# Weight loads of a two-layer attention kernel issued in the order of their readers, with the static plan of all engines drawn up anew

## The chip, the core and the metric

The kernel runs on one core of one Trainium2 chip. The metric is the device time of the whole program in microseconds (us). A core has five engines that each work through their own instruction list in order: TensorE (PE in the profile; its weight loads are PEld), ScalarE (ACT), VectorE (DVE), GpSimd (POOL) and SyncE (SP). ACT, POOL and SP also issue DMA transfers; what they spend on that is listed as ACTq and SPq, and for POOL as an operation of POOL.

## The reference, cut to what matters

```python
def attention(x, mem0, Wq, Wk, Wv, Wo, seg_len):      # x: 2048 x 512, 64 segments of 32 rows
    mem = mem0                                         # 8 x 512
    for s in range(64):
        h = concat([mem, x[segment s]])                # 40 x 512
        q, k, v = h @ Wq, h @ Wk, h @ Wv               # 32 heads of 128
        p = softmax(where(mask, q @ k.T * 128**-0.5, -1e9))
        o = (p @ v) @ Wo                               # 40 x 512
        mem = o[:8]; out += [o[8:]]
    return concat(out)
x = x + attention(layernorm(x), mem0, ...)
x = x + relu(layernorm(x) @ w1) @ w2                   # 512 -> 1376 -> 512
x = x + attention(layernorm(x), mem0, ...)             # the same weights again
x = x + relu(layernorm(x) @ w1) @ w2
```

All weights and activations are bf16, sums are f32. The segments of one layer depend on each other through `mem`, eight rows that come out of the output projection of the segment before.

## The kernel before

**Tiling and stages.** Both attention layers run at once, the second four segments behind the first (DELTA = 4), so the program has 68 steps. Step k works on segment k of the first layer and segment k-4 of the second; 80 columns hold both. A step projects queries and keys (L906, 128x128 weight tiles against 80 columns, or 40 where only one layer is active), values (L826, or L845 where only one layer is active), forms scores (L935), takes the softmax on DVE and ACT (L946 to L976), transposes the probabilities on PE (L532, `P`), copies them out twice with a mask (L999 on ACT, L1001 on DVE), multiplies with the values (L1018) and projects with Wo (L1045). L1061 copies the eight memory rows into the input `HT` of the next step. Every second step a pair of segments is finished: residual, layer norm and the dense layer (L532 and L641), as work that fits between the rest.

**Start.** All weights stay in SBUF. Wv is loaded in parts of 1, 1 and 2 MB, and Wq, Wk and Wo in two halves of 2 MB each: 16 MB. One 1 MB part of Wv is issued from SP, the eight other loads from POOL (L388, L391). While they land, PE works on groups of 128 rows of x: `prepare_group` loads a group (L678, from ACT for groups 1 to 5), normalizes it and computes its values (`late_values`), which are parked in the room of the dense weights (`w_sb` in the profile) and put to DRAM (`vh`, L802). The normalized group is put to DRAM too (`xh`, L686, from SP). `hold` (L397) is a tiny DMA from SP that reads the last head of Wo_sb; most DMAs of SP stand behind it ("loaded"), so that they do not compete with the weights.

**What sets the order.** Nothing is scheduled by hand. `Plan` records every operation with a cost for each engine that can do it, what it reads and writes, and for DMAs a lag until the data are there. `Plan.order` then simulates the engines and picks at each point, among the operations that could start soon, the one with the best priority: for PE operations `PERIOD * step + PLACE[...]`, for the rest the priority of their readers less cost, latency and `AHEAD[...]`. RULE holds four numbers of the picking rule. PLACE and AHEAD are tables of numbers found by a search. The result is one fixed list of instructions per engine. A transpose or attend operation marked EITHER is issued as one 128-column or as two 64-column matmuls, whichever leaves PE in the column mode it is in.

**How waits come about.** The framework that builds the program puts semaphore waits in front of instructions. Each DMA issued from SP or ACT signals one of eight completion semaphores, given out in turn in the order in which the program lists these DMAs. Before a DMA may use a semaphore again, its issuing engine waits until the DMA that had it before has landed. DMAs from POOL have eight semaphores of their own.

Of the kernel before, what the change touches and what calls it, by code (L numbers as in the profile page):

```python
# [24 lines left out]
       (0.13, 0.13, 0.10, 0.10, 0.20, 0.0), (1.7, 1.7, 1.7, 1.7, 1.7, 0.0), (0.3, 0.3, 0.3, 0.3, 0.3, 0.0))  # L25
# [4 lines left out]
RULE = (0.0406, 305.8805, 223.7607, 5137528097.847)  # L30
PERIOD = 51.862
PLACE = {
    ("attend.mmu0.0", 0): 464.738, ("attend.mmu0.0", 1): -761.84, ("attend.mmu1.0", 0): -48.299,
    ("attend.mmu1.0", 1): 477.592, ("attend.mmu2.0", 0): -121.389, ("attend.mmu2.0", 1): 193.039,
    ("attend.mmu3.0", 0): 108.108, ("attend.mmu3.0", 1): -173.388, ("attend.mmu4.0", 0): -138.04,
    ("attend.mmu4.0", 1): -86.354, ("dense_layer.mm.0", 1): 703.986, ("dense_layer.mm.1", 1): 23.772,
    ("dense_layer.mm.2", 1): 450.741, ("dense_layer.mm.3", 1): 440.377, ("dense_layer.mm.4", 1): 333.982,
    ("dense_layer.mm.5", 1): 738.493, ("finish_pair.turn.0", 1): 163.159, ("g0", 0): -34.469, ("g1", 0): 381.157,
    ("g2", 0): -795.105, ("g3", 0): 5.833, ("g4", 0): 32.661, ("g5", 0): 203.205, ("layernorm.turn.0", 1): 205.098,
    ("layernorm.turn.1", 1): 314.469, ("layernorm.turnr.0", 0): -1.427, ("prepare.turns.0", 0): 41.19,  # L40
    ("project.mm.0", 0): 149.221, ("project.mm.0", 1): 441.958, ("project.mm.1", 0): 706.274,
    ("project.mm.1", 1): 331.02, ("project.mm.2", 0): 669.447, ("project.mm.2", 1): 820.125,
    ("project.mm.3", 0): -204.869, ("project.mm.3", 1): -13.931, ("project.mm.4", 0): -186.279,
    ("project.mm.4", 1): -181.007, ("queries_keys.mmu0.0", 0): 5.896, ("queries_keys.mmu0.0", 1): -44.155,
    ("queries_keys.mmu0.1", 0): 34.674, ("queries_keys.mmu0.1", 1): -93.489, ("queries_keys.mmu0.2", 0): -16.377,
    ("queries_keys.mmu0.2", 1): 173.172, ("queries_keys.mmu0.3", 0): 19.391, ("queries_keys.mmu0.3", 1): -750.374,
    ("queries_keys.mmu1.0", 0): 17.611, ("queries_keys.mmu1.0", 1): -732.885, ("queries_keys.mmu1.1", 0): -106.018,
    ("queries_keys.mmu1.1", 1): -97.778, ("queries_keys.mmu1.2", 0): 41.801, ("queries_keys.mmu1.2", 1): -156.695,
    ("queries_keys.mmu1.3", 0): -179.942, ("queries_keys.mmu1.3", 1): 16.276, ("queries_keys.mmu2.0", 0): 291.119,
    ("queries_keys.mmu2.0", 1): 294.131, ("queries_keys.mmu2.1", 0): 91.208, ("queries_keys.mmu2.1", 1): 35.615,  # L50
    ("queries_keys.mmu2.2", 0): 163.031, ("queries_keys.mmu2.2", 1): 388.265, ("queries_keys.mmu2.3", 0): 189.92,
    ("queries_keys.mmu2.3", 1): 152.536, ("queries_keys.mmu3.0", 0): 82.328, ("queries_keys.mmu3.0", 1): 396.443,
    ("queries_keys.mmu3.1", 0): 54.307, ("queries_keys.mmu3.1", 1): 465.336, ("queries_keys.mmu4.0", 0): 414.302,
    ("queries_keys.mmu4.0", 1): 455.006, ("queries_keys.mmu4.1", 0): 428.286, ("queries_keys.mmu4.1", 1): 697.474,
    ("scores.mmu0.0", 0): -184.452, ("scores.mmu0.0", 1): 31.061, ("scores.mmu1.0", 0): 330.969,
    ("scores.mmu1.0", 1): -683.203, ("scores.mmu2.0", 0): -29.182, ("scores.mmu2.0", 1): -711.846,
    ("scores.mmu3.0", 0): 189.271, ("scores.mmu3.0", 1): -735.95, ("scores.mmu4.0", 0): -722.578,
    ("scores.mmu4.0", 1): 229.19, ("scores.turnu0.0", 0): 31.636, ("scores.turnu0.0", 1): 404.707,
    ("scores.turnu1.0", 0): 487.486, ("scores.turnu1.0", 1): -33.575, ("scores.turnu2.0", 0): 202.144,
    ("scores.turnu2.0", 1): -88.841, ("scores.turnu3.0", 0): -183.584, ("scores.turnu3.0", 1): -17.909,  # L60
    ("scores.turnu4.0", 0): 67.36, ("scores.turnu4.0", 1): 309.356, ("values.mm.0", 0): -186.102,
    ("values.mm.0", 1): 27.498, ("values.mm.1", 0): 32.826, ("values.mm.1", 1): 183.35,
    ("values.mm.2", 0): -107.199, ("values.mm.2", 1): 352.654, ("values.mm.3", 0): 428.105,
    ("values.mm.3", 1): -12.855, ("values.mmv0.0", 0): -89.763, ("values.mmv1.0", 0): 182.482,
    ("values.mmv2.0", 0): -173.822, ("values.mmv3.0", 0): 303.007, ("values_narrow.mm.0", 0): 182.487,
    ("values_narrow.mm.0", 1): -707.928, ("values_narrow.mm.1", 0): 164.081, ("values_narrow.mm.1", 1): -54.214,
}
AHEAD = {
    "*bulk.land": -65.074, "*late_values.put": 329.507, "*layernorm.aggr": -154.03, "*layernorm.keep": 171.765,
    "*layernorm.norm": 293.888, "*layernorm.power": 209.943, "*layernorm.stats": -173.956,  # L70
    "*prepare_group.load": -399.388, "*prepare_group.put": 280.114, "*values.ev": -52.264, "attend.ev": -169.821,
    "bulk.land": -92.619, "dense_layer.relu": 31.743, "dense_layer.relu_last": 127.159, "finish_pair.add": -113.115,
    "finish_pair.add0": -180.166, "finish_pair.add1": -44.709, "finish_pair.store": 305.649,
    "finish_pair.widen": 141.765, "late_values.put": -48.547, "layernorm.aggr": -189.08, "layernorm.keep": 259.017,
    "layernorm.norm": 2.975, "layernorm.power": 143.261, "layernorm.stats": 94.33, "load_dense.dma1": -95.621,
    "load_dense.dma2": 105.989, "load_group.get": 80.276, "load_group.load": -149.366, "load_weights.dma": -58.491,
    "load_weights.hold": 85, "make_ident": 333.562, "make_mask": -62.557, "place_values.dma": -76.842,
    "prep_x.cp": -213.044, "prepare.get_memory": -66.381, "prepare.get_x": 46.124, "prepare.keep": 225.327,
    "prepare.make_half": -61.416, "prepare.place": -66.003, "prepare.zero": 321.465, "prepare.zero_bank": -109.711,
    "prepare.zero_columns": 238.474, "prepare_group.load": 103.093, "prepare_group.put": 27.159,  # L80
    "project.ev": 229.927, "project.first": 257.853, "project.rows": -8.657, "queries_keys.ev": 381.586,
    "scores.block": 258.34, "scores.exp": -22.515, "scores.keep": 353.957, "scores.mul": 275.286,
    "scores.recip": -213.702, "scores.sub": 91.821, "scores.top": -68.377, "scores.total": 68.935,
    "values.ev": 156.514, "values_narrow.ev": -13.151,
}

LOAD, LOAD_O = 2.55, 2.9
# [8 lines left out]
def t_act(n):  # L96
    return 0.05 + 0.833e-3 * n
# [6 lines left out]
PART = {ACT: 0.13, DVE: 0.10}  # L104
# [193 lines left out]
def kernel(  # L298
# [74 lines left out]
    def bulk(eng, t, fn, name, size, r=(), w=(), rate=LOAD):  # L373

        def land():
            pass

        plan.op(eng, t, fn, r=r, w=[("issued", *name)], lag=1.5)
        plan.op(QUEUE, rate * size, land, r=[("issued", *name)], w=[*w, "queue"])
# [91 lines left out]
    def prepare():  # L471
# [34 lines left out]
        plan.available("memory", 5.0)  # L506
# [44 lines left out]
    def layernorm(x, rows, xnT, lo=0, n=128, to=None, halved=False):  # L551
# [37 lines left out]
        plan.op(POOL, 0.65, power, r=["half"], w=[ln])  # L589
# [5 lines left out]
    def dense_layer(x, rows, act):  # L595
# [4 lines left out]
        for fb in range((NFC + 3) // 4):  # L600
# [27 lines left out]
            if nfull < len(fcs):  # L628
                copy_op(n, relu_last, r=[hp], w=[hT, (hT, fb)], part=True)
# [38 lines left out]
    def prepare_group(g, gate=()):  # L668

        eng, q, t, cond = queue(g <= EARLY)  # L670
        if g == 0:
            xb = xb_tiles[0]
            plan.available(xb0, 4.0)
        else:
            xb = p_xe.buf()

            def load():
                q.dma_start(out=xb[:, :], in_=A_x[0, 128 * g:128 * (g + 1), :])  # L678

            plan.op(eng, t, load, r=[*cond, *gate], w=[xb], lag=3.5 if g <= EARLY else 2.45)  # L680
# [85 lines left out]
    def copy_op(n, fn, r, w, part=False):  # L766
        plan.op((ACT, DVE), (t_act(n) + part * PART[ACT], t_dve(n) + part * PART[DVE]), fn, r=r, w=w)
# [88 lines left out]
    def place_values(k, late):  # L856
# [6 lines left out]
        if late:  # L863
            src, key = (vg, [("vg", p) for p in range(4)]) if g == 0 else (vh[g], [("vh", g, 0), ("vh", g, 2)])
            for b in range(2):
                def dma(b=b):
                    q.dma_start(out=V0[64 * b:64 * b + HS, :, :], in_=src[64 * b + HS * c:64 * b + HS * (c + 1), :, :])

                plan.op(eng, t, dma, r=[*cond, *key], w=[("V0l", b)], lag=2.45)
            return  # L870
        for u in range(2):
            for b in range(2):
# [8 lines left out]
                plan.op(eng, t, dma, r=[*cond, *[("vw", i) for i in range(4)[src]]], w=[("V0", i, b) for i in ps], lag=2.45)  # L881
# [36 lines left out]
    def scores(k, p, xs, a_lo, a_hi, qk):  # L918
# [75 lines left out]
        for b in range(2):  # L994
# [8 lines left out]
            copy_op(n, keep, r=[tp, PT, "half"], w=[(PT, b)])  # L1003
# [175 lines left out]
```

## Time and profile before

| what | value |
|---|---|
| time, median of 3 runs | 1670.47 us (1670.08 to 1671.12) |
| the profiled execution's own time | 1670.9 us |
| its span, first to last instruction | 1669.2 us |
| mean granted TensorE clock | 0.992 |
| PE busy | 1605.1 us, 96% of the span, 40146 matmul records |
| PEld, DVE, ACT, POOL busy | 82%, 66%, 63%, 10% |
| DMA | 64.26 MB, mean 38 GB/s |

PE is busy 96% of the span, so a microsecond of PE work or of PE waiting is a microsecond of the result, save where the start or the end of the program is bound by transfers. Because matmuls overlap in the array, the busy share alone doesn't show how densely they follow each other; the time from the start of one matmul to the start of the next does. "Position" below means the sum of these start-to-start times along PE's instruction list, without any waiting: for 80 columns 36 ns, for 40 columns 25 ns, for 512 columns 216 ns (two 64-column matmuls share one such slot), and 96 ns more at each change between 128-, 64- and 32-column mode. All are medians of this trace.

### The profile page before, as it was taken

To read this page: it belongs to the slowest core of one execution; us is meant where nothing else is said; L and a number is where in the kernel's file an instruction comes from. 1 tells how busy PE (TensorE), PEld (TensorE's weight loads), DVE (VectorE), ACT (ScalarE), POOL (GpSimd) and SP (SyncE) were. 2 spreads that over 40 slices of the span, in tenths; PEclk is the share of its full clock that TensorE was granted. 3 is DMA by queue.
4 is the path that set the end of the run, shared out by engine and by line. 5 is a ranking of instruction groups with operands and counts; after the bars stand their busy time and mean duration, and the time that the engine had idled before them with its cause. 6 is when DMAs were issued, how large, how long until landed. Compare 5 with 4: busy or idle time off the path is not lost.

```text
span 1669.2 us, 88991 instructions
## 1 busy us (share of the span) xinstructions
PE 1605.1 (96%) x40146; PEld 1376.4 (82%) x40206; DVE 1098.7 (66%) x3043; ACT 1051.7 (63%) x2662; POOL 160.0 (10%) x387
## 2 busy tenths in 40 slices
PE   4899999999999999999999999999999999999997
PEld 2688888888888888888888888888888888888886
DVE  3457667666766766676676677667667666766765
ACT  2567666666666666666676666666666666666664
POOL 3010010100100010010000101000010100001000
PEclk8999999999999999999999999999999999999999
DMA  9621011010101010110010110011010000000000
GB/s 352 223 53 29 18 28 28 24 36 20 29 26 28 25 31 24 27 26 27 27 27 25 31 32 25 16 35 27 25 37 19 22 25 26 18 18 18 18 5 7
DMA packets 35487, 64.26 MB, mean 38 GB/s; under 512 B 7226, under 2 KB 19234, under 8 KB 35106
## 3 DMA queue, kind: packets, MB, share of 16 engines
q1 hardware_dynamic: 29218, 39.09, 8.7%
q0 software_dynamic: 4704, 18.35, 2.9%
q8 instruction: 315, 5.16, 1.3%
q10 hardware_dynamic: 1184, 1.12, 0.2%
q14 instruction: 66, 0.54, 0.1%
HBM read 33.50 MB, written 11.93 MB: 27 GB/s over the span
## 4 chain that ended last, share of the span: by engine, by line
PE 82%; DVE 12%; issue 2%; DMA 2%; ACT 1%; ACTq 0%; POOL 0%; POOLq 0%; DVEq 0%
PE work L906 34%; PE st L1045 18%; PE fill L826 14%; PE fill L532 7%; PE work L1018 4%; PE work L935 3%; DVE PT L1001 3%; PE work L532 2%; DVE mx L950 2%; DVE es L953 2%; DMA Wq_sb<-in_A_Wq_dram 2%; DVE es L946 1%; DVE sm L960 1%; DVE OT L764 1%; DVE P L976 1%
## 5 line engine op out<-in xcount | busy, mean ns | idle before, releaser
L906 PE MATMUL work<-HT,Wk_sb 128*128 128x80 bf16 (+1 forms) x8704 | 368.6, 199 | 11.8 <-DVE HT L1061 11.1
L906 PE MATMUL work<-HT,Wq_sb 128*128 128x80 bf16 (+1 forms) x8704 | 362.4, 200 | 11.5 <-DMA Wq_sb<-in_A_Wq_dram 11.3
L906 PEld LDWEIGHTS <-Wk_sb 128*128 128x128 bf16 x8704 | 329.8, 99 | 37.9 <-issue 27.2
L906 PEld LDWEIGHTS <-Wq_sb 128*128 128x128 bf16 x8704 | 325.8, 100 | 25.0 <-issue 13.4
L1045 PE MATMUL st<-OT,Wo_sb 128*128 128x80 bf16 (+1 forms) x8704 | 342.7, 200 | 3.7 <-issue 1.9
L1045 PEld LDWEIGHTS <-Wo_sb 128*128 128x128 bf16 x8704 | 319.0, 100 | 17.0 <-issue 13.0
L762 ACT CAST kT<-work 128x320 bf16<-128x320 f32 (+1 forms) x539 | 223.3, 414 | 96.2 <-PE work L906 60.3
L762 ACT CAST qT<-work 128x320 bf16<-128x320 f32 (+1 forms) x509 | 209.5, 412 | 84.9 <-PE work L906 38.1
L826 PE MATMUL fill<-Wv_sb,HT 128*64 128x512 bf16 x2048 | 254.6, 380 | 0.0
L762 ACT CAST vw<-fill 128x512 bf16<-128x512 f32 x233 | 136.5, 586 | 147.2 <-PE fill L826 143.1
L762 ACT CAST OT<-work 128x320 bf16<-128x320 f32 (+1 forms) x411 | 160.5, 426 | 97.5 <-PE work L1018 97.4
L1001 DVE TENSOR_SCALAR PT<-work,half 128x320 bf16<-128x320 f32 (+2 forms) x357 | 172.2, 493 | 18.6 <-PE work L532 13.6
L946 DVE TENSOR_TENSOR es<-work,maskb 128x320 f32<-128x320 f32 (+2 forms) x340 | 133.3, 401 | 54.1 <-PE work L935 52.7
L826 PEld LDWEIGHTS <-HT 128*64 128x64 bf16 x2048 | 99.9, 109 | 68.0
L999 ACT ACTIVATE PT<-work,half 128x160 bf16<-128x160 f32 (+2 forms) x323 | 127.3, 430 | 37.3 <-PE work L532 26.6
L953 DVE TENSOR_TENSOR es<-es,mx 128x320 f32<-128x320 f32 (+2 forms) x340 | 145.9, 438 | 5.3
L957 ACT ACTIVATE es<-es 128x320 f32<-128x320 f32 (+2 forms) x340 | 134.1, 406 | 20.6 <-DVE es L953 17.3
L960 DVE TENSOR_REDUCE sm<-es 128x8 f32<-128x320 f32 (+2 forms) x340 | 131.2, 395 | 12.9 <-ACT es L957 11.6
L950 DVE TENSOR_REDUCE mx<-es 128x8 f32<-128x320 f32 (+2 forms) x340 | 132.6, 399 | 5.6
L728 DVE TENSOR_TENSOR xg<-xg,fill 128x512 f32<-128x512 f32 (+1 forms) x34 | 23.4, 688 | 166.1 <-PE fill L532 161.5
L1061 DVE CAST HT<-st 128x64 bf16<-128x64 f32 (+1 forms) x67 | 14.8, 221 | 171.5 <-PE st L1045 171.5
L976 DVE TENSOR_TENSOR P<-es,sm 128x160 bf16<-128x160 f32 (+1 forms) x304 | 121.0, 409 | 4.1
(91 smaller groups left out, 1833.2 us busy)
## 6 DMA issues: line engine op xcount, KB each, us to landing
V<-vw SPq DMA_DIRECT2D x252, 48.0 KB
V<-vh SPq DMA_DIRECT2D x120, 64.0 KB
vh<-vg SPq DMA_DIRECT2D x20, 256.0 KB
Wo_sb<-in_A_Wo_dram POOLq DMA_DIRECT2D x2, 2048.0 KB, 24.8
Wk_sb<-in_A_Wk_dram POOLq DMA_DIRECT2D x2, 2048.0 KB, 29.0
Wq_sb<-in_A_Wq_dram POOLq DMA_DIRECT2D x2, 2048.0 KB, 32.6
Wv_sb<-in_A_Wv_dram POOLq DMA_DIRECT2D x1, 2048.0 KB, 12.1
vh<-w_sb POOLq DMA_DIRECT2D x4, 512.0 KB, 9.7
```

Source lines behind the costliest of these rows:

```text
L532: nc.tensor.matmul(out_[u:v, :], lhsT=lhsT[:, u:v], rhs=rhs, start=start, stop=stop, tile_position=(0, u))
L762: nc.scalar.copy(out=out_, in_=in_)
L826: nc.tensor.matmul(vp[64 * b:64 * b + 64, :], lhsT=cols(c4), rhs=Wv_sb[:, c4, n * 512:(n + 1) * 512], start=(c4 == 0), stop=(c4 == NC4 - 1 ...
L906: nc.tensor.matmul(qp[:, hi * 2 * L:hi * 2 * L + n], lhsT=W_sb[:, c4, h * Dh:(h + 1) * Dh], rhs=HT[:, c4, c0:c1], start=(c4 == 0), stop=(c ...
L946: nc.vector.tensor_tensor(out=flat(es[:, A]), in0=flat(sp[:, A]), op=ALU.add, in1=maskb[:, a_lo:a_hi, :].unsqueeze(2).to_broadcast([128, n ...
L950: nc.vector.tensor_reduce(out=mx[:, As], in_=es3(), axis=AX.X, op=ALU.max)
L953: nc.vector.tensor_tensor(out=es3(), in0=es3(), op=ALU.subtract, in1=mx[:, As].unsqueeze(2).to_broadcast([128, ns * na, L]))
L957: nc.scalar.activation(out=es[:, A], in_=es[:, A], func=ACTF.Exp, scale=SCALE)
L960: nc.vector.tensor_reduce(out=sm[:, As], in_=es3(), axis=AX.X, op=ALU.add)
L976: (nc.gpsimd if eng == POOL else nc.vector).tensor_tensor(out=o, in0=flat(es[:, A]), op=ALU.mult, in1=sm[:, As].rearrange("p (a s) -> p a ...
L1001: nc.vector.tensor_scalar_mul(out=o, in0=i, scalar1=half[:, b:b + 1])
L1045: nc.tensor.matmul(wo[:, 2 * W * c4 + c0:2 * W * c4 + c1], lhsT=Wo_sb[:, h, c4 * 128:(c4 + 1) * 128], rhs=OT[:, h, c0:c1], start=(h == 0 a ...
```

## The change

No operation is added or taken away, and no arithmetic changes. What changes is the input of the planner, and so the order of the program.

- Weight loads issued from POOL now write a common key ("issue"), so POOL issues them in the order in which the code lists them. Before, the planner was free.
- Costs are altered: time per MB of weights 2.55 to 2.68 (Wo 2.9 to 2.95), lags of early loads of x from 3.5 to 6.0 and of the placement of values into V0 from 2.45 to 6.0 (step 0) and 4.5 (steps 1 and 2), 1.5 from issue on POOL or SP to the transfer queue in the latency table in place of a lag on the operation, 0.80 in place of 0.65 for the power on POOL, 0.11 (ACT) and 0.065 (DVE) more for the masked copies, later times for the first x and the memory.
- RULE, PERIOD, PLACE and AHEAD hold other numbers.

The core of the diff (the tables are left out):

```diff
-       (0.13, 0.13, 0.10, 0.10, 0.20, 0.0), (1.7, 1.7, 1.7, 1.7, 1.7, 0.0), (0.3, 0.3, 0.3, 0.3, 0.3, 0.0))
+       (0.13, 0.13, 0.10, 0.10, 0.20, 1.5), (1.7, 1.7, 1.7, 1.7, 1.7, 1.5), (0.3, 0.3, 0.3, 0.3, 0.3, 0.0))
-RULE = (0.0406, 305.8805, 223.7607, 5137528097.847)
-PERIOD = 51.862
+RULE = (0.0747, 374.3032, 410609.8064, 1181571967619443.75)
+PERIOD = 67.7026
...
-LOAD, LOAD_O = 2.55, 2.9
+LOAD, LOAD_O, SLOW = 2.68, 2.95, 6.0
...
-PART = {ACT: 0.13, DVE: 0.10}
+PART, MASKED = {ACT: 0.13, DVE: 0.10}, {ACT: 0.11, DVE: 0.065}
...
-        plan.op(eng, t, fn, r=r, w=[("issued", *name)], lag=1.5)
+        plan.op(eng, t, fn, r=r, w=[("issued", *name), *(["issue"] if eng == POOL else [])])
         plan.op(QUEUE, rate * size, land, r=[("issued", *name)], w=[*w, "queue"])
...
-            plan.op(eng, t, load, r=[*cond, *gate], w=[xb], lag=3.5 if g <= EARLY else 2.45)
+            plan.op(eng, t, load, r=[*cond, *gate], w=[xb], lag=SLOW if g <= EARLY else 2.45)
...
-                plan.op(eng, t, dma, r=[*cond, *key], w=[("V0l", b)], lag=2.45)
+                plan.op(eng, t, dma, r=[*cond, *key], w=[("V0l", b)], lag=SLOW if k == 0 else 4.5 if k < 3 else 2.45)
...
-            copy_op(n, keep, r=[tp, PT, "half"], w=[(PT, b)])
+            copy_op(n, keep, r=[tp, PT, "half"], w=[(PT, b)], more=MASKED)
```

The issue order of the weight loads from POOL, in the two built programs (in the new file, lines after the tables stand one lower: L906 is L907 there):

| | 1 | 2 | 3 | 4 | 5 | 6 | 7 | 8 |
|---|---|---|---|---|---|---|---|---|
| before | Wv 1 MB | Wv 2 MB | Wo 2nd half | Wk 1st | Wq 1st | Wo 1st | Wk 2nd | Wq 2nd |
| changed | Wv 1 MB | Wv 2 MB | Wq 1st | Wk 1st | Wq 2nd | Wk 2nd | Wo 1st | Wo 2nd |

In the built program of the changed kernel, the DMA issues and copies of ACT around the fifth early load of x stand as follows (in brackets what each waits for beside its own buffers; HW and SW are the completion semaphores of DMAs of SP and ACT, and of POOL):

```
SP    held<-Wo_sb                      [SW7: the last weight load, Wo 2nd half]   signals HW7
ACT   V<-vw x4                         [HW1, HW3]                                 signals HW1 to HW4
ACT   qT0 copy
ACT   V<-vg x2                         [HW5, HW6]                                 signals HW5, HW6
ACT   qT3 copy, xg copy (group 2)
ACT   xe<-x, group 5                   [HW7]                                      signals HW7
ACT   xg copy (group 3)                its reader on PE: L827, 193rd matmul
```

In the program before, `held` waits for the third load of POOL and signals HW5, the fifth early load of x waits for HW6, which an early load before it signals, and the next user of HW5 is the second `V<-vw` of step 0.

Over the whole program, PE has 40206 matmuls before and 40624 after (418 transposes and attends more are split into two 64-column ones), and changes its column mode 366 and 373 times. Of the operations that more than one engine can do, 35 multiplications of L976 leave POOL for DVE, 110 masked copies (L999, L1001) leave DVE for ACT, and on balance 139 other copies leave ACT for DVE, 31 of `hT`, 29 each of `vw`, `OT` and `kT` among them; ACT has 29 operations less in all and DVE 64 more.

## The prediction

> **What bounds the kernel now.** I read the page first: PE is busy 96% of the span, so the rest of the program matters where it makes PE wait. The table by stretches, cut at the start, shows where that is (columns: stretch, length, busy time and instructions of PE, PEld, DVE, ACT, POOL, granted clock, DMA share, GB/s).
>
> ```profile
> 26.00:35.20 9.20, 0.00 (x0) 0.00 (x0) 0.00 (x0) 0.00 (x0) 0.00 (x0) 0.50 1.04 364
> 35.20:39.70 4.50, 4.46 (x78) 3.42 (x80) 1.11 (x3) 1.46 (x4) 0.37 (x2) 0.50 1.02 350
> 39.70:49.00 9.30, 9.30 (x152) 5.61 (x150) 0.41 (x1) 6.47 (x14) 1.57 (x3) 1.00 1.02 407
> ...
> 600.00:800.00 200.00, 196.81 (x4870) 169.12 (x4875) 138.57 (x372) 130.91 (x323) 19.11 (x47) 1.00 0.10 28
> ```
>
> Nothing computes for nine microseconds at the start while the DMA engines are full, and PE restarts at half clock. In the middle PE is dense. The waits and the timeline name what the start waits for (waits: total, times, longest; timeline: start, length, idle before).
>
> ```profile
> PE work L906 <- DMA Wq_sb<-in_A_Wq_dram: 11.3, 2, 10.5
> ...
> PE work L906 <- DVE HT L1061: 11.1, 36, 0.3
> ```
> ```profile
> 22.35 0.32 SPq L397 DMA_DIRECT2D held<-Wo_sb  x1
> ...
> 24.72 0.54 ACTq L678 DMA_DIRECT2D xe<-in_A_x_dram  x1
> ...
> 35.23 1.78 PE L906 MATMUL work<-HT,Wq_sb 128*128 128x40 bf16 x48 [10.53 <-DMA Wq_sb<-in_A_Wq_dram]
> ```
> ```profile
> SPq L397 <- DMA Wo_sb<-in_A_Wo_dram: 21.1, 1, 21.1
> ```
>
> PE waited 10.5 us for the fifth weight load. The tiny `held` waited on SP until 22.35, when the third load was in, and all SP work stood behind it. Note this line: it is harmless here.
>
> The transfers' times from issue to landing (tile views of the weights: minimum, median, maximum of two) give all landings: Wo at 4.1 + 18.2 = 22.3 and 41.1, Wk at 28.5 and 46.2, Wq at 8.9 + 26.3 = 35.2 and 12.7 + 38.8 = 51.5. Wv is whole at 3.3 + 12.1 = 15.4. So loads land in the order of issue, 5.1 to 6.9 us each, whichever they are.
>
> ```profile
> DMA to landing us min/median/max: 26.3/32.6/38.8
> ```
>
> Summing start-to-start times (position, as above) gives 1566.5 us for PE's whole list, mode changes included. The span has about 103 us more: 42.6 are lost by the end of step 3, 44.7 in steps 4 to 63, 11.3 after. In the middle, rounding of the unit times and matmuls missing from the trace account for some 12 of the 44.7; waiting proper is about 33 us, of which 14.4 are the 0.48 us before every second step's first query block (the memory rows through L1061).
>
> **The change, part by part.**
>
> *Order of the loads.* Wq's first half becomes the third load from POOL and lands at about 22.3 in place of 35.2; PE's 10.5 us wait has no ground any more. This alone would be a gain. Wo's halves go last. The last load lands when 16 MB have passed: 51.5 before. Before 51.5, two more puts of values (L802, 0.5 MB each, issued at 43.3 and 46.8) shared the engines; the changed program can make only one put that early, so I take 0.5 to 1 MB less at 377 GB/s: Wo whole at 50.2 (49 to 51.6).
>
> *What is queued behind that.* `held` reads the last head of Wo. Before, this was the third load; now it is the last. In the order of the changed program, `held` takes completion semaphore HW7, and the next DMA to take HW7 is ACT's fifth early load of x. ACT must wait there until `held` has landed, and ACT works in order. Behind it on ACT stands the copy of group 3's transposed rows (`xg`), and PE's 193rd matmul (L827, values of group 3) reads that copy. PE is in order too. On DVE the statistics of group 5 wait for the same load, with the first softmax behind them. None of these waits exists in the trace before: there the early load was issued at 24.72 while `held` was over.
>
> When does PE stop? At position 12.77. It cannot be later than about 28: it reaches Wq's first block near 25 in both programs (position 9.06 before, 9.76 now), has its weights by then, and 3.0 us of work are left. When does it start again? Wo in at 50.2; `held` issued in 0.3 (its row: 0.32) and landed. That landing is not in the trace. Near rows: a 256 KB put takes 2.5 from issue to landing, the second early load of x, amid the weights, 5.9. [...] By [...] the loaded row 3.4 later. Since `held` starts when the queue has just run dry, I take 2.5: 53.0. Then ACT's DMA issue of 0.54, the copy of 0.59 and hops of 0.1: PE restarts at 54.3 (52.5 to 58).
>
> Before, PE reached this position at 40.5 (the first two 0.86 us blocks of that group end at 39.7 and 40.5; ACT's copies at 39.86 and 40.72 show it). Delay: 54.3 - 40.5 = 13.8 us.
>
> *Clock after the pause.* After its 10.5 us pause PE ran at half clock for 4.5 us (row 35.20:39.70); at the very start, from 10.7 until 19.2, for 8.5 us. The skill page "TensorE: Matmul & The Clock Gate" ("What's actually happening") says that one busy window of about 3.4 us restores the clock; that would cost 1.7 us. The rows give 2.2 to 4.3; both exceed the rule. The pause is now 26 us or more, so I take 3. From 40.5 to the end of step 0 (68.5) the kernel before lost 4.8 us, 2.6 of it around the four DMA issues on ACT between 49.4 and 54.9 and 0.8 for Wq's second half. Those issues now lie before the pause, and all weights are in. I leave 2.3 for dependences and get 5.3 with the clock: 0.5 more. Start in sum: 13.8 + 0.5 = **+14.3 us** at the end of step 0. For steps 1 to 3 I assume the same loss as before (10.7 us, with the dense weights' load in step 1): SP's list there has nearly the same entries, and all of it shifts with step 0.
>
> *SP and POOL.* SP's stores of `xh` now also wait for 50.2 behind `held`; the first reader is step 4, so nothing is late. POOL issues the same eight loads; `ident` moves ahead of five of them, which can start PE up to 1.5 us earlier and is lost in the pause.
>
> *Mode changes and splits.* 373 in place of 366 changes at 96 ns: +0.7 us. Two 64-column matmuls start 35 ns apart as a pair, one 128-column matmul takes 36: the 418 splits cost nothing.
>
> *Where copies run.* DVE gains 35 x 0.41 + 139 x 0.5 and loses 110 x 0.49: about +30 us, 66% to 68% of the span. ACT loses about 15. Neither becomes the bound; their cover is the slack between producer and reader on PE.
>
> *Middle.* For each PE operation I compared PE's position between producer and reader with the durations of the copies and softmax steps between them, from their rows. Summed over steps 12 to 59 the shortage is 28.7 us before (the trace has about 27 of waiting there) and 26.4 after, once a shortage hidden behind the wait just ahead of it is left out. The 0.48 us wait for the memory rows is still there at every second step. Scaled to 60 steps: -2.9 us. Queueing on ACT and DVE can add to this and not take away; bounds -4 and +8.
>
> *End.* In the last four steps more dense-layer and value blocks stand between the dependent operations; the shortage falls by a third. Of 5.3 us lost there I take off 2 (0 to 4). The last 13 us, a pure chain, are unchanged.
>
> Sum: 14.3 + 0.7 - 2.9 - 2.0 = +10.1. On the profiled execution's 1670.9 us (1669.2 of span and 1.7 around it) that gives **1681 us**; the median of the runs is 0.4 lower, which changes nothing.
>
> **Rivals.**
>
> 1. *The wait on ACT does not bind (not slower).* If the early load passed in time, PE would run through step 0 with weights landing just ahead of it, bounded by Wo at 50.2 and half of L1045 after it: step 0 ends near 54 and not 68.5. With the rest as above: 1670.9 - 14.5 - 4.2 = **1652**. For it: the landings; each weight would be there when PE comes to it. Against it: the program's order, which gives `held` and this load one semaphore, and the SP row above, where an engine stood 21.1 us for one landing with all its list behind. It decides at the point where the restart comes before 44.2 (54.3 less 10.1): then the saving elsewhere wins.
> 2. *The wait binds, but the new tables save more in the middle (no change).* To cancel +10.1, 10 of the 33 us of waiting would have to go beyond what I took off: about **1669**. Against it: the memory wait stays, and it is nearly half of the total.
> 3. *The middle gets worse.* DVE at 68% and its longer queue delay a softmax step by 0.15 us in each of 60 steps: +9, so **1690**. For it: many readers stand less than 0.5 us behind their data, as many as before. Against it: the planner now has dearer, more truthful copies.
>
> **How the numbers follow.** The main case gets 0.77, rival 1 0.09, rival 2 0.07, rival 3 0.07. The main case's own range is 1673 to 1689: restart -2 to +4, clock 1, middle -1 to +5, end 2. From 1669 to 1691 the range leaves out rival 1 and part of rival 3 and of the edges. A measurement of this kernel tells about 0.2% (3.3 us) from no change. Slower by more: nearly all of the main case, rival 3, 0.82; within: 0.09 (rival 2 and the low edge); faster: 0.09.
>
> **What would show it.** In the changed profile PE must be idle from about 27 to 54 with the copy of `xg` on ACT right behind a DMA issue of L679 at about 53, and `held` issued near 50. Wq's first half must make no wait. Half clock should follow for 4 to 8 us, and step 0's last L1046 near 83. If ACT issues the fifth early load before 30, the main step is wrong. If steps 4 to 63 differ by more than 8 us from before, the reading of the middle is.

## The result, and the profile after

| what | before | changed |
|---|---|---|
| time, median of 4 runs | 1670.28 us (1669.28 to 1671.12) | 1660.82 us (1660.03 to 1661.40) |
| ratio, 95% interval | | 0.9943 (0.9926 to 0.9961) |
| span of the profiled execution | 1669.2 us | 1659.4 us |

The kernel became 0.57% faster. The forecast was 1681, slower, with a range from 1669 to 1691: the sign is wrong, and the time lies 8 us below the range.

The start first. The table by stretches of the changed kernel, cut at its pause (columns as in the prediction):

```profile
20.00:27.30 7.30, 4.42 (x88) 2.89 (x86) 3.35 (x8) 1.07 (x3) 1.49 (x4) 0.94 1.03 382
27.30:54.50 27.20, 0.92 (x6) 0.04 (x2) 0.00 (x0) 0.59 (x2) 0.00 (x0) 0.50 0.92 323
54.50:60.00 5.50, 5.46 (x80) 3.35 (x82) 0.70 (x1) 2.23 (x6) 0.00 (x0) 0.50 0.25 75
60.00:82.00 22.00, 20.88 (x447) 15.08 (x443) 10.22 (x45) 13.90 (x35) 4.48 (x9) 0.99 0.27 101
600.00:800.00 200.00, 198.98 (x5024) 172.29 (x5023) 145.16 (x385) 132.90 (x325) 16.60 (x40) 1.00 0.11 28
```

Where PE paused for 10.5 us before, it now pauses for 26.3. Half clock follows until 60.5, so the row from 60.00 on has a mean of 0.99. The last row is the middle: PE is busy for 198.98 of 200 us, where before it was 196.81.

The timelines of SP, ACT and PE of the changed kernel show what ended the pause (start, length, idle before and its releaser):

```profile
52.39 0.32 SPq L398 DMA_DIRECT2D held<-Wo_sb  x1
```
```profile
53.52 0.34 ACTq L679 DMA_DIRECT2D xe<-in_A_x_dram  x1
53.91 0.59 ACT L763 CAST xg<-fill 128x512 bf16<-128x512 f32 x1 [27.64 <-DMA held<-Wo_sb]
```
```profile
54.55 1.92 PE L827 MATMUL fill<-Wv_sb,xg 128*64 128x512 bf16 x8 [26.33 <-ACT xg L763]
```

This is the forecast chain link by link: the last weight load, `held`, the fifth early load of x on ACT, the copy of `xg`, PE. The waits of SP and DVE agree, the second being the statistics of the early groups:

```profile
SPq L398 <- DMA Wo_sb<-in_A_Wo_dram: 51.1, 1, 51.1
```
```profile
DVE ln L560 <- DMA xe<-in_A_x_dram: 35.7, 5, 31.1
```

So the start did lose nearly what was said, and the program gained more elsewhere. Lost time (time less position, at PE's last output projection of a step; the first row is contained in the second):

| stretch | before | changed | difference | forecast |
|---|---|---|---|---|
| to the end of step 0 | 32.0 | 45.6 | +13.6 | +14.3 |
| to the end of step 3 | 42.6 | 54.7 | +12.1 | +14.3 |
| steps 4 to 63 | 44.7 | 23.9 | **-20.8** | **-2.9** |
| after step 63 | 11.4 | 9.5 | -1.8 | -2.0 |
| position of the whole list | 1566.4 | 1567.1 | +0.7 | +0.7 |
| sum | | | -9.8 | +10.1 |

The sum, without the first row, is the difference of the spans. The 4.1 us from the start of PE's last matmul to the end of the span are the same in both kernels and stand in no row. Nearly all of the miss is in one row.

### The profile page after: what moved, and what is told of

It reads as the page before. It is cut to its first block, busy times and chain, and to the rows that moved or that the text cites. A ratio compares the mean times of both kernels' runs of the same rounds, so it can differ in the third digit from the quotient of the medians.

```text
span 1659.4 us, 89728 instructions
## 1 busy us (share of the span) xinstructions
PE 1595.7 (96%) x40624; PEld 1371.5 (83%) x40624; DVE 1122.4 (68%) x3107; ACT 1049.3 (63%) x2633; POOL 146.1 (9%) x352
## 4 chain that ended last, share of the span: by engine, by line
PE 93%; DMA 3%; DVE 2%; ACT 1%; issue 1%; POOL 0%; ACTq 0%; POOLq 0%; DVEq 0%
PE work L907 37%; PE st L1046 18%; PE fill L827 16%; PE fill L533 11%; PE work L1019 4%; PE work L936 4%; DMA Wo_sb<-in_A_Wo_dram 2%; PE work L533 2%; ACT OT L763 0%; DVE HT L1062 0%; PE fill L642 0%; DMA xe<-in_A_x_dram 0%; PE fill L846 0%; ACT PT L1000 0%; ACT es L958 0%
## 5 line engine op out<-in xcount | busy, mean ns | idle before, releaser
L907 PE MATMUL work<-HT,Wq_sb 128*128 128x80 bf16 (+1 forms) x8704 | 368.3, 200 | 9.9 <-DVE HT L1062 9.1
L907 PE MATMUL work<-HT,Wk_sb 128*128 128x80 bf16 (+1 forms) x8704 | 363.3, 200 | 0.0
L907 PEld LDWEIGHTS <-Wq_sb 128*128 128x128 bf16 x8704 | 327.5, 99 | 36.2 <-DVE HT L1062 18.7
L907 PEld LDWEIGHTS <-Wk_sb 128*128 128x128 bf16 x8704 | 324.8, 100 | 16.8 <-issue 14.6
L763 ACT CAST kT<-work 128x320 bf16<-128x320 f32 (+1 forms) x510 | 208.9, 410 | 79.1 <-PE work L907 34.5
L1000 ACT ACTIVATE PT<-work,half 128x320 bf16<-128x320 f32 (+2 forms) x433 | 189.7, 465 | 55.0 <-PE work L533 34.4
L947 DVE TENSOR_TENSOR es<-work,maskb 128x320 f32<-128x320 f32 (+2 forms) x340 | 134.5, 404 | 110.9 <-PE work L936 94.7
L763 ACT CAST OT<-work 128x320 bf16<-128x320 f32 (+1 forms) x382 | 152.1, 415 | 62.7 <-PE work L1019 62.2
L763 ACT CAST vw<-fill 128x512 bf16<-128x512 f32 x204 | 119.3, 585 | 90.1 <-PE fill L827 81.9
L977 DVE TENSOR_TENSOR P<-es,sm 128x320 bf16<-128x320 f32 (+2 forms) x339 | 132.2, 406 | 3.4
L1002 DVE TENSOR_SCALAR PT<-work,half 128x320 bf16<-128x320 f32 (+2 forms) x247 | 108.7, 448 | 23.2 <-PE work L533 22.5
L936 PEld LDWEIGHTS <-qT 128*40 128x40 bf16 x4096 | 86.2, 98 | 45.5 <-ACT qT L763 2.4
```

Of the source, the lines that this page charges most:

```text
L763: nc.scalar.copy(out=out_, in_=in_)
L907: nc.tensor.matmul(qp[:, hi * 2 * L:hi * 2 * L + n], lhsT=W_sb[:, c4, h * Dh:(h + 1) * Dh], rhs=HT[:, c4, c0:c1], start=(c4 == 0), stop=(c ...
L936: nc.tensor.matmul(v[64 * g2:64 * g2 + L, a, i, b, :], lhsT=qT[:, hi, a * L:(a + 1) * L], rhs=kT[:, hi, a * L:(a + 1) * L], start=True, st ...
L947: nc.vector.tensor_tensor(out=flat(es[:, A]), in0=flat(sp[:, A]), op=ALU.add, in1=maskb[:, a_lo:a_hi, :].unsqueeze(2).to_broadcast([128, n ...
L977: (nc.gpsimd if eng == POOL else nc.vector).tensor_tensor(out=o, in0=flat(es[:, A]), op=ALU.mult, in1=sm[:, As].rearrange("p (a s) -> p a ...
L1000: nc.scalar.activation(out=o, in_=i, func=ACTF.Copy, scale=half[:, b:b + 1])
```

## What the traces tell of the middle

No kernel beyond these two was run. What follows is worked out from the two traces and from the orders of operations that the planner gives. It is a reading, not a test by an intervention, and the end of this section says what would have tested it and wasn't tried.

**Which waits went.** For each pair of neighbouring matmuls between 150 and 1600 us, I took the time from start to start less the usual one for its kind. The excess, in us, by the operation that had to wait:

| who waits | before | changed |
|---|---|---|
| transposes of probabilities (L532, `P`) | 15.4 | 3.2 |
| attend (L1018) | 9.3 | 0.1 |
| first query block, for the memory rows (L906) | 14.4 | 13.1 |
| output projection (L1045) | 4.6 | 6.7 |
| rest | 2.1 | 2.9 |
| sum | 45.8 | 26.0 |

(12.6 us of the excess before are left out: they are 58 matmuls that have no record in that trace, all in the dense layer.) The memory wait is still there, as forecast; where the page of waits before has 11.1 us in 36 waits (shown in the prediction), the changed kernel has (us, times, longest)

```profile
PE work L907 <- DVE HT L1062: 9.1, 29, 0.3
```

What disappeared are the waits for the softmax and for the masked copies: 21.4 of 24.7 us. The trace attributes them partly to PE's weight loads, since these fetch `P`. For the multiplication that ends the softmax, who waited for it in the kernel before (us, times):

```profile
PEld L532: 13.6, 47
PE work L532: 5.9, 12
```

and in the changed kernel:

```profile
PEld L533: 2.9, 10
PE work L533: 0.3, 2
```

**Is the softmax faster, or is PE's order roomier?** Two readings fit these lines.

- *Engine:* 110 masked copies left DVE for ACT, and 35 multiplications left POOL, where they took 0.72 us, for DVE at 0.51 (320 columns). So the softmax and the copies end earlier.
- *Room:* the new order of PE puts more work between a unit's scores and the transposes of its probabilities, and between these and attend. The data may take as long as before.

The multiplications on POOL can be struck out as direct causes: of the 60 waits before in which a transpose starts within 90 ns after the end of such a multiplication, all 60 follow one on DVE.

For the rest I took, for each of the five units of steps 6 to 62 (285 cases), the latency from the last score matmul to the end of the multiplication, hops included, and the room: the time that PE had other things to do in between, its waiting for this unit left out. Then I exchanged the two between the kernels. A shortage is latency less room where positive, summed over all cases (us; a mean of each in the first two columns; for attend the 29 cases of unit 4 in even steps are left out, as a missing record makes their start uncertain):

| | mean latency, before and changed | mean room, before and changed | shortage before | changed | latencies before, rooms changed | latencies changed, rooms before |
|---|---|---|---|---|---|---|
| P transposes | 4.66, 4.78 | 5.02, 5.31 | 15.0 | 2.4 | 9.5 | 50.1 |
| attend | 1.39, 1.38 | 2.03, 2.27 | 9.7 | 0.0 | 0.0 | 17.0 |

The latencies did not fall; the softmax takes 0.12 us longer in the mean. The rooms grew by 0.29 and 0.24 us. The old latencies with the new rooms give 9.5 of 24.7 us; the new latencies with the old rooms would give 67. So the new rooms alone would remove most of it, and the new latencies with the old rooms would remove nothing in sum. The exchange treats the two as independent, which they are not: a new order moves both. That makes the last column overstate: in odd steps unit 3's scores come earlier on PE, so their softmax queues longer on DVE (3.26 to 4.67 us) and has more room (3.08 to 4.97); 38.4 of the 50.1 are this one case. For attend it is unit 0 of odd steps, 13.3 of the 17.0: its latency grew by 0.57 us and its room by 0.97. Without these two cases, about 22 us of shortage stood before; the new rooms alone would leave 9.5 of them, the new latencies alone about 15. So room did more, and the shorter latencies would by themselves have taken about a third, nearly all of it at the attend of unit 1 in even steps, shown below. One place speaks for the engine alone: unit 4 of odd steps, where the latency fell from 3.51 to 3.03 while its room shrank from 3.42 to 3.30; with the old latency it would lack 7.0 us there, not 1.2.

**One of the cases, in the traces.** In even steps of the kernel before, unit 1's attend waits about 0.28 us each time, some 8 us in sum. Step 30, DVE:

```profile
770.87 1.10 DVE L953 TENSOR_TENSOR es<-es,mx 128x320 f32<-128x320 f32 x2
771.90 0.48 DVE L764 CAST OT<-work 128x320 bf16<-128x320 f32 x1
772.30 0.54 DVE L1001 TENSOR_SCALAR PT<-work,half 128x320 bf16<-128x320 f32 x1
```

and PE:

```profile
772.13 0.67 PE L532 MATMUL fill<-xnM,w_sb 128*64 128x128 bf16 x18
772.89 0.23 PE L1018 MATMUL work<-PT,V 128*64 128x80 bf16 x2
```

The transposes were out at 770.88. The second masked copy stood behind two other DVE operations, began at 772.30 and ended at 772.83; attend began 0.05 later. Both readings are in this one: the copy queued, and PE had only 1.75 us of other work. In the changed kernel both copies of the same unit run on ACT:

```profile
773.73 0.94 ACT L1000 ACTIVATE PT<-work,half 128x320 bf16<-128x320 f32 x2
```

They end at 774.67, and attend comes at 776.56: the latency fell from 2.02 to 1.18, the room rose from 1.75 to 3.00. Either alone would have ended the wait, so this third of the 24.7 us does not decide between the two readings.

**Which part of the change gives the room?** The planned orders say where it does not come from, though not what it is worth in time. With the planner's own costs, which give PE's time without any waiting, the mean distance on PE from scores to transposes is 4.96 us before and 5.35 in the changed kernel. With the chain of the weight loads alone it stays 4.96. With all new costs and the old tables it is 5.16, with 370 mode changes. With the new tables and the old costs it is 4.54, with 475 mode changes, 109 more than before, at 96 ns some 10 us of PE's list. So the new costs with the old tables give about half of the gain in distance, the new tables with the old costs none, and only both together give all of it. Why is not shown.

**What wasn't tried.** Moving only the masked copies between ACT and DVE, with PE's list unchanged, in either kernel: it would decide between engine and room directly. The two mixtures above, for their times. And a tiny SP transfer that reads the fifth early tile of x, put ahead of `held`: the early load then takes a semaphore whose earlier owner has long landed, while PE's list stays the same. If the pause goes, step 0 can end when Wo is in and half the projection done, near 55 in place of 81.7. By this estimate some 25 us are there for the taking in the changed kernel; no run shows it.

## Why the prediction was wrong, point by point

- *Order of the loads and the restart: right.* Wq made one wait of 0.5 us in place of 10.5, and PE restarted at 54.55 (forecast 54.3). Two terms inside missed in opposite ways. Wo was in at 52.4 and not 50.2 (in part because the transfers ran at 348 GB/s between 40 and 50 us, not at the 377 taken); from the issue of `held` to ACT's next issue it took 1.13 us, not 2.8. The near row, a put of 256 KB, was too long for a transfer of 32 bytes.
- *Clock: right in size, wrong in the reason.* The clock record has half speed until 60.53, 6.0 us after the restart, which costs 3.0, forecast 3. The forecast took a longer pause to mean a longer return, and set aside the rule of the skill page "TensorE: Matmul & The Clock Gate" ("What's actually happening"), one busy window of about 3.4 us, since that would cost 1.7. But the page also says that the window runs freely, whatever the kernel does, and both traces fit that. The changes of the granted clock between 26 and 102 us (before at 26.02, 39.67, 84.04 and 90.87; changed at 26.39, 60.53, 98.07 and 101.49) lie whole multiples of 3.41 us apart in each trace. On that grid the first window that PE filled runs from 36.26 to 39.67 before and from 57.12 to 60.53 in the changed kernel, and each time the clock came back at its end. By these figures the return takes one window and what is left of the one in which PE restarts: 4.4 and 6.0 us.
- *Steps 0 to 3 after the restart: slightly too dear.* From 54.55 to 81.69, PE lost 3.8 us (forecast 5.3), and steps 1 to 3 lost 9.1 (assumed as before, 10.7).
- *Mode changes, splits, end: right,* +0.7 and -1.8.
- *Middle: wrong, and the step that turned the sign.* The prediction gave 8 us of difference in steps 4 to 63 as the sign that its reading of the middle is wrong; it was 20.8. Three statements carried the reading. First, "waiting proper is about 33 us": the 12 us of missing records had been taken off a loss in which they don't count. Lost time was matched with the full list of matmuls, so a missing record loses nothing. The real waiting was 45.8. Second, "the trace has about 27 of waiting there", which made the calculated 28.7 look calibrated. With the right figure it is 45.8 x 48 / 60 = 36.6, so the calculation was 8 us short. Third, what was short: the latencies were sums of bare durations. For the transposes and attend they gave 5.8 us in 48 steps, scaled 7.2, where the trace has 24.7. What the bare sums leave out is the queueing in front of the operations, on DVE as in step 30 above; how much of the missing 17.5 us it is was not measured apart. The text then said that queueing "can add to this and not take away". But queueing that is in the kernel before can be covered by the order after, and it was.
- *The size of it.* The calculation was 7.9 us too low before (28.7 against 36.6) and 5.6 too high after (26.4 against 26.0 x 48 / 60 = 20.8). Together that is 13.5 in 48 steps, 16.9 in 60; with the forecast 2.9 it makes 19.8, which is 45.8 less 26.0.
- *What a better sum would have given.* The old latencies with the new rooms give -15.2 us for transposes and attend where the bare sums gave (1.0 - 5.8) x 60 / 48 = -6.0. That is 9 us less, a forecast near 1672: no change. The rest would still have been missed. This is an estimate with hindsight, because the new rooms are those of the changed kernel's trace; the order known beforehand has nearly their mean (5.35 us in the planner's costs, 5.31 in the trace), but what it gives case by case was not worked out.
- *Rivals.* Rival 1 fell as expected: the wait on ACT bound. Rival 2, the middle saves more, is what happened, with 18 us beyond the sum where it needed 10. "Nearly half of the total" stays as memory wait was the argument against it; of 45.8 it was under a third. Rival 3, a busier DVE, had the right sign for the latency (0.12 us longer in the mean, forecast 0.15), and it cost nothing, as the room grew by more.

One sum of the prediction does not close: its "about 103 us more" than the position is listed as 42.6, 44.7 and 11.3, which is 98.6. The rest is the 4.1 us after PE's last matmul. They are the same in both kernels and change nothing.

DVE's load did rise as forecast, to 68%. The page's row for the first softmax operation, before and changed, shows that DVE has more idle time in front of it, though, most of it for the scores:

```profile
L946 DVE TENSOR_TENSOR es<-work,maskb 128x320 f32<-128x320 f32 (+2 forms) x340 | 133.3, 401 | 54.1 <-PE work L935 52.7
L947 DVE TENSOR_TENSOR es<-work,maskb 128x320 f32<-128x320 f32 (+2 forms) x340 | 134.5, 404 | 110.9 <-PE work L936 94.7
```

It waited 52.7 us for the scores before and 94.7 now. DVE, which has slack, waits more, and PE, which has none, waits less.

## What to carry to other kernels

In an in-order pipeline, compare the latency that the trace shows between producer and reader, queueing included, with the work that stands between them in the reader's order; bare durations hide the very waits that a new order can remove. Before a residue is called noise, count it in one way only: missing records shorten a sum of records, not a difference of times. And a tiny transfer that waits for the last load can hold a whole engine through the reuse of a completion semaphore, so look at which transfer owned it before.

## What the runs showed of the hardware

- The transfer of 32 bytes to DRAM had landed, and the waiting engine had gone on, 1.13 us after the start of its issue (52.39 to 53.52), with the queue nearly empty. The skill page "DMA: Bandwidth & Descriptors" ("Anatomy of one DMA — SWDGE (gpsimd) path") has about 2.0 us fixed, but for transfers that GpSimd issues; this one was issued from SP.
- The full clock came back 4.4 us after PE's restart in the kernel before and 6.0 us after it in the changed one. Both times it was the end of the first 3.41 us window that PE filled, counted on the grid of the clock's own changes. At the start of the kernel before it was so too: PE's long runs began at 10.72, with a gap of 0.68 us before 15.45, and full clock came at 19.19, the end of the window from 15.78.
